# Forward Q and K projections as four column groups of 32 rows, with the memory rows batched over eight segments and Q and K kept token-major in DRAM

## The chip, the cores and the metric

The kernel runs on one core of one Trainium2 chip. The metric is the device time in microseconds (us) of one execution of the whole kernel, forward and backward in one launch. Each run also left one execution taken by the hardware profiler; all readings below are from such executions. "Granted clock" is the share of full speed that the throttle allowed TensorE.

The engines are named as the profile names them: PE is TensorE (PEld its weight loads), DVE is VectorE, ACT is ScalarE, POOL is GpSimd, SP is SyncE, whose queue here does nothing but issue DMAs.

## The reference

A memory-augmented recurrent attention, a residual, a SwiGLU feed-forward layer, and the gradients of all of it. Only the attention matters here: 64 segments run one after the other, because the first 8 output rows of a segment are the memory rows of the next.

```python
# S=2048 tokens, D=448, H=16 heads, Dh=256, M=8 memory rows, seg_len=32, L=40 rows in a segment
mem = mem0
for s in range(64):
    h = concatenate([mem, x[:, 32*s : 32*s + 32]], axis=1)       # 40 rows
    q = einsum('btd,dhe->bhte', h, Wq); k = ... Wk; v = ... Wv    # each 448 x 4096
    scores = where(mask, einsum('bhqe,bhke->bhqk', q, k) * scale, -1e9)
    p = softmax(scores)
    o = einsum('bhqk,bhke->bhqe', p, v)
    o = einsum('bhte,hed->btd', o, Wo)
    mem = o[:, :8]                                                # the recurrence
    outs.append(o[:, 8:])
h = x + concat(outs);  out = h + swiglu(layernorm(h));  gradients by vjp
```

The memory rows of a segment are known only at the very end of the segment before. The kernel lays the 40 rows out with the memory rows last: the 32 rows `M:L` are 24 tokens and the 8 memory rows, and the 8 rows `0:M` are tokens, which are known long before. That is what the change uses.

## The kernel before

The sequence of one forward segment. Weights are the stationary operand, the 40 rows of the segment the moving one, so Q and K come out with the feature on the partitions and need no transpose:

```python
def wpass(W_sb, s, dst, hb, eng):                     # 64 matmuls in two banks; four calls a segment
    for x in range(2):
        ps = k.ps1()
        for j in range(j0, j0 + 8):
            for kc in range(KC):                      # KC = 4 chunks of 128 rows; the last holds 64, padded with zeros
                nc.tensor.matmul(ps[:, (j-j0)*L:(j-j0+1)*L],                    # L432
                    lhsT=W_sb[:, kc, c*P:(c+1)*P], rhs=hT_roll[:, kc, sl, :], ...)
        k.evac(dst[:, j0:j0+8, 0:L], ...)             # L75 on VectorE, L76 on ScalarE

# one segment s
wpass(Wq_sb, s, qT, 0, "vs"); wpass(Wk_sb, s, kT, 0, "sv"); wpass(Wq_sb, s, qT, 1, "vs")
pS0 = scores(0)                                       # L500 mask, L505 scores
softmax(0, pS0)                                       # L512 to L518, VectorE and ScalarE
wpass(Wk_sb, s, kT, 1, "sv")
value_rows(0)                                         # L527, V: 8 matmuls 128x512 in two column groups, x4
pS1 = scores(1); softmax(1, pS1)
value_rows(1); transposed_p(0); value_rows(2)         # L536
values(0); transposed_p(1); value_rows(3)             # L548
out_proj(0, 8); values(1); out_proj(8, MC)            # L561, four column groups of 32 rows
to_s = nc.scalar.copy(out=om[0:64, :], in_=pO[64:P, 0:256])        # L589: "om", once a segment
to_v = nc.vector.tensor_tensor(out=om2[0:64, :], ...)              # L590
... nc.tensor.transpose(...)                                       # L596, memory rows turned
to_v = nc.vector.tensor_copy(out=hT_roll[..., SEG:L], ...)         # L597, into the next segment's rows
# (cut) stores for the backward: feature-major Q and K, padded from 40 to 64 columns, 512 KB each
nc.gpsimd.dma_start(out=dr["QT"][s], in_=qT...)
nc.sync.dma_start(out=dr["KT"][s], in_=kT...)
nc.sync.dma_start(out=dr["VG"][s], in_=Vs)
```

In the backward, each segment loads Q, K and V with transposing DMAs, and every 16th segment stores a block of memory-row gradients (`DHb`) on the queue that also loads `DH` for the layer norm's backward:

```python
def load_seg(s):
    load_v(s)                                                       # transposing load of VG
    nc.sync.dma_start_transpose(out=Q_sb, in_=dr["QT"][s])
    nc.sync.dma_start_transpose(out=K_sb, in_=dr["KT"][s])
    ...
# each backward segment: ... nc.vector.tensor_copy(out=om[:, 0:224], in_=pH[:, 0:224])   # L990 "omb"
if jm == 0:                                                         # jm = s % 16
    nc.sync.dma_start_transpose(out=dhx, in_=dmr...)                # L1009
    nc.gpsimd.dma_start(out=dr["DHb"][r0:r0+P, :], in_=dhx...)      # L1011
if r == 0:                                                          # r = s % 4
    ...
    nc.gpsimd.dma_start(out=dh_h, in_=dr["DH"][rows, c0:c0+224])    # L1052, in ln_bwd (L260)
```

`with tc.issue_after(x):` places what is inside it behind instruction `x` in the scheduler's order; otherwise a list scheduler puts the instructions of each engine, DMAs included, in one order. That an issue stands behind an earlier one of its engine is seen in the timelines below: in the changed kernel a store whose data was ready at 335.80 us was issued on SyncE's queue at 352.84, behind a DMA whose buffer came free at 349.60.

## Time and profile before

Before the prediction the kernel's time was 3364.26 us (median of three runs, 3356.36 to 3373.26). I cut the profiled execution into stages by the start of ScalarE's copy L589 (one per forward segment) and VectorE's L990 (one per backward segment):

| stage, kernel before | us |
|---|---|
| start to the end of segment 0 | 54.5 |
| 63 forward segments | 1111.1, mean 17.64, median 16.97, lowest 16.12 |
| feed-forward layer, to the first backward segment | 398.9 |
| 63 backward segments | 1084.7, mean 17.22, median 16.76 |
| weight gradients and the rest | 721.4 |

The page's first and second parts and its instruction queue: busy time and its share of the span, then busy tenths in 40 equal slices, the granted clock in tenths, and packets, MB and share of the 16 DMA engines.

```profile
PE 2994.7 (89%) x56532; PEld 2021.4 (60%) x56532; DVE 1306.7 (39%) x3309; ACT 1036.2 (31%) x2501; POOL 727.8 (22%) x1507
...
PE   5888888988988869886999999999999589999998
...
PEclk8999999999999989997999999999999799999999
...
q8 instruction: 442, 7.24, 0.9%
```

TensorE is busy in eight or nine tenths of most slices, so the work on TensorE and what TensorE waits for set the time. One forward segment without a disturbance, from the timeline of PE (start, duration, line, output<-input, shape of the operands, matmuls in the group, and in brackets the idle time before and who ended it):

```profile
97.34 4.96 PE L432 MATMUL psf<-arA,arW 128*128 128x40 bf16 x192 [0.27 <-DVE arA L597]
102.14 0.23 PE L500 MATMUL psf<-arB,ident 128*128 128x160 bf16 x1
...
102.67 1.77 PE L432 MATMUL psf<-arA,arW 128*128 128x40 bf16 x64
104.37 1.05 PE L527 MATMUL psf<-arW,arA 128*64 128x512 bf16 x8
...
110.49 1.49 PE L561 MATMUL po<-arW,arA 128*32 128x256 bf16 x48
112.97 0.23 PE L596 MATMUL psf<-ident,arB 64*128 64x64 bf16 x2 [0.98 <-DVE arB L590]
113.46 0.31 PE L432 MATMUL psf<-arA,arW 128*128 128x40 bf16 x6 [0.26 <-DVE arA L597]
```

Subtract starts, not durations, since the records of two groups overlap (97.34 + 4.96 = 102.30, and the next group starts at 102.14): Q and K take 4.80 + 1.70 = 6.50 us, and the segment 113.46 − 97.34 = 16.12 us. This is the lowest of the 63. The mean is 1.5 us more, and the list of waits of PE between 60 and 1160 us (us in total, times, longest) says what part of that is:

```profile
PE psf L596 <- DVE arB L590: 49.9, 50, 1.6
PE psf L432 <- issue: 40.4, 24, 4.7
```

"issue" is time in which TensorE waited for nothing that the profile shows. In the backward (1564 to 2649 us), the wait of PE and then of DVE:

```profile
PE po L972 <- DVE arA L75: 23.6, 15, 7.3
```

```profile
DVE arB L260 <- DMA arB<-DH: 49.3, 15, 7.5
```

### The profile page before, as it was taken

Reading aid. Unit: us, or ns where it says so; the run is one execution under the profiler, and the core shown is the slowest. Engines: PE = TensorE matmul, PEld = TensorE weight load, DVE = VectorE, ACT = ScalarE, POOL = GpSimd, SP = SyncE. Lnnn points to the kernel's source line nnn. Section 1 sums busy time; section 2 is a strip of 40 time slices with the busy share of each in tenths; the row PEclk is TensorE's granted clock in tenths of the full one; section 3 lists DMA queues with packets and bytes.
Section 4 is the critical chain, followed back from the end, with each engine's and each line's share of the span. In section 5 each row is a group of like instructions: output and inputs, shape, how many; then the busy total and the mean of one; then the engine's idle time right before and its main releaser. Section 6 shows DMA issues by size and latency. Waiting matters only on the chain.

```text
span 3370.6 us, 124942 instructions
## 1 busy us (share of the span) xinstructions
PE 2994.7 (89%) x56532; PEld 2021.4 (60%) x56532; DVE 1306.7 (39%) x3309; ACT 1036.2 (31%) x2501; POOL 727.8 (22%) x1507
## 2 busy tenths in 40 slices
PE   5888888988988869886999999999999589999998
PEld 4666666676766646664666666666666344444443
DVE  4344344344344357773444444444444201111110
ACT  2333333333333323332333333333333101020110
POOL 3222222122121212121222222122211212112111
PEclk8999999999999989997999999999999799999999
DMA  7656865777665698987777878887877967979952
GB/s 271 188 158 182 220 165 159 182 183 204 175 183 159 211 240 198 200 209 238 162 169 160 168 158 180 157 168 163 174 164 171 287 190 210 201 183 195 198 146 69
DMA packets 998890, 623.49 MB, mean 185 GB/s; under 512 B 900868, under 2 KB 912788, under 8 KB 995860
## 3 DMA queue, kind: packets, MB, share of 16 engines
q1 hardware_dynamic: 921428, 361.57, 51.6%
q0 software_dynamic: 76928, 253.93, 22.8%
q8 instruction: 442, 7.24, 0.9%
q14 instruction: 92, 0.75, 0.1%
HBM read 125.38 MB, written 271.52 MB: 118 GB/s over the span
## 4 chain that ended last, share of the span: by engine, by line
PE 68%; issue 10%; DVE 9%; DMA 7%; ACT 3%; POOL 1%; SPq 1%; ACTq 0%; POOLq 0%; DVEq 0%
PE psf L432 12%; PE po L972 8%; PE psf L1149 8%; PE psf L929 5%; PE psf L527 4%; PE psf L906 4%; PE po L561 3%; PE psf L1170 3%; PE fx L1031 3%; PE psf L710 2%; PE fx L800 2%; PE psf L994 2%; PE fx L1154 2%; DVE arA L75 2%; PE psf L548 2%
## 5 line engine op out<-in xcount | busy, mean ns | idle before, releaser
L76 ACT CAST arA<-psf 128x320 bf16<-128x320 f32 (+5 forms) x1267 | 519.1, 425 | 1491.0 <-PE psf L432 390.1
L75 DVE CAST arA<-psf 128x320 bf16<-128x320 f32 (+5 forms) x1093 | 489.2, 464 | 1016.6 <-PE psf L1149 259.2
L432 PE MATMUL psf<-arA,arW 128*128 128x40 bf16 x16384 | 450.8, 181 | 81.1 <-issue 41.8
L432 PEld LDWEIGHTS <-arW 128*128 128x128 bf16 x16384 | 439.9, 97 | 90.3 <-issue 67.4
L972 PE MATMUL po<-arW,arA 128*32 128x448 bf16 x6144 | 360.9, 365 | 47.8 <-DVE arA L75 43.6
L527 PE MATMUL psf<-arW,arA 128*64 128x512 bf16 x2048 | 275.6, 394 | 4.7 <-DMA arW<-in_A_Wv_dram 2.8
L1149 PE MATMUL psf<-arW,arA 128*128 128x512 bf16 x1030 | 259.5, 379 | 0.0
L972 PEld LDWEIGHTS <-arA 128*32 128x32 bf16 x6144 | 155.1, 98 | 168.5 <-DVE arA L75 46.5
L1149 PEld LDWEIGHTS <-arA 128*128 128x128 bf16 x1440 | 136.0, 98 | 164.8 <-issue 13.7
L929 PEld LDWEIGHTS <-arW 128*128 128x128 bf16 x8192 | 213.8, 96 | 28.9 <-issue 28.9
L929 PE MATMUL psf<-arA,arW 128*128 128x40 bf16 x8192 | 217.9, 180 | 10.1 <-DVE arA L998 5.1
L710 PE MATMUL psf<-arW 128*128 128x256 bf16 x1344 | 155.9, 277 | 50.3 <-DMA arW<-arW 38.5
L710 PEld LDWEIGHTS <-arW 128*128 128x128 bf16 x1344 | 133.1, 99 | 75.0 <-issue 37.3
L527 PEld LDWEIGHTS <-arA 128*64 128x64 bf16 x2048 | 109.6, 113 | 64.1 <-issue 12.3
L561 PE MATMUL po<-arW,arA 128*32 128x192 bf16 (+1 forms) x4096 | 136.7, 262 | 5.9 <-DMA arW<-in_A_Wo_dram 5.0
L76 ACT CAST arB<-psf 40x160 bf16<-40x160 f32 (+3 forms) x448 | 120.9, 270 | 35.3 <-DVE arB L75 25.6
L906 PEld LDWEIGHTS <-arW 128*128 128x128 bf16 x2048 | 88.9, 101 | 66.3 <-issue 63.4
L939 ACT COPY arA<-psf 128x1024 bf16<-128x1024 bf16 x128 | 123.3, 1015 | 2.2 <-PE psf L938 0.4
L561 PEld LDWEIGHTS <-arA 128*32 128x32 bf16 x4096 | 96.1, 96 | 40.7 <-DVE arB L75 20.2
L1170 PEld LDWEIGHTS <-arW 128*128 128x128 bf16 x606 | 60.1, 99 | 98.7 <-DMA arW<-X_o 36.6
L75 DVE CAST arB<-psf 40x160 bf16<-40x160 f32 (+3 forms) x384 | 108.5, 296 | 22.5 <-PE psf L536 22.5
L906 PE MATMUL psf<-arB,arW 128*128 128x80 bf16 x2048 | 100.0, 204 | 16.1 <-DVE arB L956 6.1
(272 smaller groups left out, 3848.9 us busy)
## 6 DMA issues: line engine op xcount, KB each, us to landing
QT<-arA POOLq DMA_DIRECT2D x64, 512.0 KB, 4.6
KT<-arA SPq DMA_DIRECT2D x64, 512.0 KB, 4.2
VG<-arA SPq DMA_DIRECT2D x64, 512.0 KB, 3.8
X_o<-arA POOLq DMA_DIRECT2D x40, 512.0 KB, 5.5
X_v<-arA POOLq DMA_DIRECT2D x32, 512.0 KB, 6.7
X_k<-arA POOLq DMA_DIRECT2D x32, 512.0 KB, 4.1
X_q<-arA POOLq DMA_DIRECT2D x32, 512.0 KB, 4.4
arW<-X_o SPq DMA_DIRECT2D x30, 512.0 KB, 14.5
```

Source lines behind the costliest of these rows:

```text
L75: return nc.vector.tensor_copy(out=out, in_=in_)
L76: return nc.scalar.copy(out=out, in_=in_)
L432: nc.tensor.matmul(ps[:, (j - j0) * L:(j - j0 + 1) * L], lhsT=W_sb[:, kc, c * P:(c + 1) * P], rhs=hT_roll[:, kc, sl, :], start=(kc == 0), ...
L527: nc.tensor.matmul(pV[64 * g:64 * g + 64, 0:512], lhsT=hT_flat[:, kc, sl * L:sl * L + 64], rhs=Wv_sb[:, kc, n * 512:(n + 1) * 512], start= ...
L561: nc.tensor.matmul(pO[32 * q:32 * q + 32, 0:w], lhsT=xblk[:, j, r * SEG:(r + 1) * SEG], rhs=Wo_sb[:, cj(j), 256 * dh:256 * dh + w], start= ...
L710: nc.tensor.matmul(ps[:, f2 * 256:(f2 + 1) * 256], lhsT=Wt[:, kc, c * P:(c + 1) * P], rhs=xT[:, kc, :], start=(kc == 0), stop=(kc == KC - 1))
L906: nc.tensor.matmul(ps[b][:, i * 2 * L:(i + 1) * 2 * L], lhsT=lhs[:, cl, :], rhs=rhs_bd[:, cl // 2, :, :].rearrange("p g n -> p (g n)"), st ...
L929: nc.tensor.matmul(pss[b][:, jj * L:(jj + 1) * L], lhsT=WoT_sb[:, kc, c * P:(c + 1) * P], rhs=do_roll[:, kc, sl, :], start=(kc == 0), stop ...
L939: nc.scalar.copy(out=dO_sb[:, 8 * hf:8 * hf + 8, :], in_=ph.rearrange("p (c n) -> p c n", n=P))
L972: nc.tensor.matmul(pH[32 * (j % 4):32 * (j % 4) + 32, 0:D], lhsT=blk[nm][:, j, r * SEG:(r + 1) * SEG], rhs=WT[:, cj(j), :], start=(nm == " ...
L1149: nc.tensor.matmul(pa[2 * kc + g][:, 0:w], lhsT=lhs_of(b)[:, kc * P:(kc + 1) * P], rhs=rhs_of(b, g), start=(b == 0), stop=(b == nblk - 1), ...
L1170: nc.tensor.matmul(pa[i][:, 0:D], lhsT=lhs_of(b, i), rhs=rhs_of(b), start=(bi == 0), stop=(bi == len(nblk) - 1))
```

## The change

The intent is to make Q and K with fewer TensorE instructions. The 32 rows `M:L` become the stationary operand, four copies of it in four column groups of the array, and the weights the moving one, 512 columns at a time; the last, half-filled chunk of the contraction runs Q's part in rows 0 to 63 and K's part in rows 64 to 127 of the array together (in the trace after, the eight such matmuls of a block start within 23 ns). The result is token-major and has to be turned back by 16 TensorE transposes. The other 8 rows, known early, are projected for 8 segments at once with 64 moving columns, spread over the segments before, and GpSimd copies 8 of the columns into each segment's Q and K. V's last chunk is halved the same way. In DRAM, Q and K are now stored token-major (`T1q`, `T1k` per segment, `T0q`, `T0k` per 8 segments), so that the backward loads them with plain DMAs in place of transposing ones, and V is stored in 80 rows in place of 128.

The core of the diff (cut: allocation, start-up, V, the order within the segment):

```diff
-    def wpass(W_sb, s, dst, hb, eng):   # (shown above)
+    qk_st = A(15, 2, 2, 512)                                   # one staging buffer for all segments
+    def qk_rows(s, b):
+        banks = [k.ps1(), k.ps1()]
+        for w in range(2):
+            for kc in range(KC - 1):
+                for q in range(4):                             # four column groups
+                    nc.tensor.matmul(banks[w][32*q:32*q+32, :], lhsT=hT_roll[:, kc, sl, M:L],
+                                     rhs=(Wq_sb, Wk_sb)[w][:, kc, col(q, b)], ...)          # L465
+        for q in range(4):
+            for w in range(2):                                 # half chunks: row group w, column group q
+                last = nc.tensor.matmul(banks[w][32*q:32*q+32, :], lhsT=hT_roll[64*w:64*w+64, KC-1, sl, M:L],
+                                        rhs=Wqk3[64*w:64*w+64, col(q, b)], ...)             # L469
+        for w in range(2):
+            k.evac(qk_st[:, w, b, :], banks[w][:], "vs"[w])
+    def qk_turned(s, b):                                       # 8 transposes, L479, two copies
+        ...
+    def rest_rows(s):                                          # GpSimd: 8 columns into Q and K, L424
+        ...
+            qk_rows(s, 0); qk_rows(s, 1)
+            qk_turned(s, 0); value_rows(0)
+            pS0 = scores(0); softmax(0, pS0)
+            qk_turned(s, 1); value_rows(1); value_rest(0)      # L578, half chunks of V L586
+            ...
+            out_proj(8, MC)
+            if bm < NSEG // 8 - 1:                             # bm, bu = divmod(s, 8)
+                for u in (...): rest_unit(bm + 1, u)           # 32 matmuls of 64 columns, L413
-        nc.gpsimd.dma_start(out=dr["QT"][s], in_=qT.rearrange("p c n -> p (c n)"))
-        nc.sync.dma_start(out=dr["KT"][s], in_=kT.rearrange("p c n -> p (c n)"))
+        for w, nm in enumerate("qk"):
+            nc.sync.dma_start(out=dr["T1" + nm][s], in_=qk_st[:, w]...)                     # L672
-        nc.sync.dma_start(out=dr["VG"][s], in_=Vs)
+        for g in range(2):
+            nc.sync.dma_start(out=dr["VG"][s, L*g:L*g+L], in_=Vs[64*g:64*g+L, :])           # L675
+        if bu == 2 + bm % 2:
+            for w, nm in enumerate("qk"):
+                ot = stg()
+                nc.sync.dma_start_transpose(out=ot..., in_=R_b[bm % 2][w]...)               # L685
+                nc.gpsimd.dma_start(out=dr["T0" + nm][bm], in_=ot)
@@ load_seg (backward)
-        nc.sync.dma_start_transpose(out=Q_sb, in_=dr["QT"][s])
-        nc.sync.dma_start_transpose(out=K_sb, in_=dr["KT"][s])
+        for nm, T_sb in (("q", Q_sb), ("k", K_sb)):
+            t1 = dr["T1" + nm][s]...; t0 = dr["T0" + nm][s // 8]...
+            for g in range(2):
+                for src, i0, i1 in ((t1[g], M, L), (t0[s % 8, g], 0, M)):
+                    nc.sync.dma_start(out=T_sb[64*g+i0:64*g+i1]..., in_=src)
```

## The prediction

> **What bounds the kernel.** The chain of waits is TensorE for 68% and "issue" for 10%. By ScalarE's copy of the output projection (one per segment), the forward recurrence runs to 1166 us: segment 0 ends at 55 us, 63 more take 17.6 us each. FFN runs to about 1545, backward to 2640, weight gradients to the end.
>
> **An undisturbed forward segment** (timeline from 97.3 us) takes 16.1 us of TensorE issue time:
>
> | part | us |
> |---|---|
> | Q and K, 256 matmuls 128x40 at 25 to 26.6 ns | 6.5 |
> | V, 32 matmuls | 4.0 |
> | mask, scores, P transposes, values | 2.3 |
> | output projection, 64 in four column groups | 1.9 |
> | wait for om, turn of memory rows | 1.5 |
>
> The mean is 1.5 us more. The list of waits gives L432 40 us of "issue" (24 stalls, up to 4.7 us). The instruction queue moved 7.24 MB, about 64 bytes per TensorE instruction; I read the stalls as fetch falling behind 512 instructions in 6.5 us.
>
> **After, per segment.**
> - Q and K: two blocks of six rounds of four 32x512 matmuls. The backward's four-group 448-column matmuls take 204 ns a round (43 in 2.19 us), so I estimate 230 ns at 512. The eight half-chunk matmuls: 0.35 us, estimated. Sum 3.5. [...] this trace shows column groups only (48 output-projection matmuls in 1.40 us).
> - 16 transposes at 61 ns (L938): 1.0.
> - Other 8 rows: 32 matmuls of 64 columns, about 35 ns each (between 25 at 40 columns and 46 at 80): 1.1, largely inside the om wait.
> - V: 3.6.
>
> TensorE instructions fall from 840 to 550 a segment, and their fastest burst goes.
>
> Against it: VectorE gains two casts 128x512 (685 ns), two bf16 copies (about 400), two V casts and a remainder copy, and loses four casts at 489: +2 us, between two softmaxes whose chain from scores to P is 2.16 us. Laid end to end with trace durations, TensorE waits for V's bank (0.25), P (0.3, then 0.9 for the second half), value copies (0.6) and the first rows (0.5). I get 16.2 us undisturbed (15.9 to 16.7): no shorter than now. The gain should come from lost stalls: 16.6 on average, a forward of 1100 us, saving 60 to 70.
>
> **Backward.** Two of three large transposing loads per segment become plain loads of 2 KB rows. Q and K have about 15 us to land. VectorE's 42 us of waits for DH loads and TensorE's 16 us behind VectorE may shrink: 10 us. FFN and gradients: unchanged.
>
> **Prediction:** 3285 us, 80% range 3215 to 3345. Faster by over 2%: 0.57; within 2%: 0.36; slower: 0.07.
>
> **What would show it.** Segment spacing 16.2 to 16.8; Q/K rounds near 230 ns; half chunks under 0.5 us a block; forward "issue" under 15 us; a wait near 0.9 us of the second P transposes for VectorE; backward shorter by 0 to 20 us.
>
> **What would make it wrong.** GpSimd now copies the other 8 rows into Q and K on its in-order queue, behind DMA issues that wait for transposes (140 us today); if late, scores wait. Row groups that serialize add up to 1 us a segment. If the stalls have another cause, they stay: "same". If VectorE overlaps better, 15.5 us a segment and near 3220.

## The result, and the profile after

The changed kernel took 3275.43 us (median of four runs, 3272.35 to 3282.10), the kernel before in the same rounds 3368.76 (3356.36 to 3374.21). A ratio in this document is the mean time of one kernel's fast runs over the mean of the other's fast runs of the same rounds, so it is not quite the ratio of the medians quoted. It is 0.9731 here, with a 95% interval of 0.9697 to 0.9764: faster by 2.7%. The time is 10 us from the predicted 3285 and inside the range.

The stages, cut the same way (by L654 and L1074), show that it was not reached in the predicted manner:

| stage | before | after | measured change | predicted change |
|---|---|---|---|---|
| to the end of segment 0 | 54.5 | 59.3 | +4.8 | in the next line |
| 63 forward segments | 1111.1 | 1065.6 | −45.6 | −60 to −70 |
| lowest forward segment | 16.12 | 15.11 | −1.01 | none (16.2) |
| mean forward segment | 17.64 | 16.91 | −0.72 | about −1.0 (16.6) |
| forward segments over 18.5 us | 17 | 10 | −7 | no number given |
| feed-forward layer | 398.9 | 392.7 | −6.2 | 0 |
| 63 backward segments | 1084.7 | 1035.0 | −49.7 | −10 (0 to −20) |
| weight gradients and the rest | 721.4 | 727.8 | +6.4 | 0 |

How far may one such profile be trusted? A second profile of the changed kernel (the control run below) had a forward of 1056.5, a feed-forward stage of 401.8 and a backward of 1032.8. The kernel before repeats less well: its forward, unchanged in four of the runs below, took 1104.5 to 1118.4 us there, and its backward, unchanged in e7_before_fwd_plain, 1092.9 against 1084.7. So I don't read a difference under 14 us between single forward stages, nor one under 10 us between single feed-forward or backward stages.

The same lines of the page after:

```profile
PE 2935.2 (89%) x47442; PEld 1763.0 (54%) x47442; DVE 1393.8 (42%) x3497; ACT 1030.0 (31%) x2437; POOL 761.7 (23%) x1716
...
PE   6889898988988869995999999999999499999998
...
PEclk9999999999999989997999999999999799999999
...
q8 instruction: 372, 6.09, 0.8%
```

TensorE's busy time fell by only 60 us. An undisturbed segment of the changed kernel, again from PE's timeline:

```profile
541.48 1.48 PE L465 MATMUL psf<-arW,arA 128*32 128x512 bf16 x24 [0.27 <-DVE arA L664]
542.89 0.41 PE L469 MATMUL psf<-arW,arA 64*32 64x512 bf16 x8
543.23 1.48 PE L465 MATMUL psf<-arW,arA 128*32 128x512 bf16 x24
544.63 0.41 PE L469 MATMUL psf<-arW,arA 64*32 64x512 bf16 x8
544.98 0.62 PE L479 MATMUL psf<-ident,arA 128*128 128x128 bf16 x8
...
552.11 0.28 PE L596 MATMUL fx<-ident,arB 128*40 128x40 bf16 x8 [0.66 <-DVE arB L568]
...
554.81 1.10 PE L413 MATMUL fx<-arA,arW 128*128 128x64 bf16 x32
555.87 0.20 PE L660 MATMUL psf<-ident,arB 64*128 64x64 bf16 x1
...
556.59 0.40 PE L465 MATMUL psf<-arW,arA 128*32 128x512 bf16 x4 [0.27 <-DVE arA L664]
```

Both Q/K blocks take 544.98 − 541.48 = 3.50 us. The other rows (L413) fill the 1.06 us in which the kernel before waited 0.98 us for "om", and the memory rows' turn (L660) follows them with no idle time. All of one undisturbed segment, start to start, each row summed over its groups in the timeline:

| part, us | before | after | predicted for after |
|---|---|---|---|
| Q and K matmuls | 6.50 | 3.50 | 3.5 |
| transposes of Q and K | – | 1.09 | 1.0 |
| V | 3.98 | 4.13 | 3.6 |
| mask and scores | 0.97 | 0.68 | |
| P transposes and values | 1.15 | 1.29 | |
| output projection | 2.05 | 1.98 | |
| other 8 rows | – | 1.06 | 1.1 |
| wait for om | 0.98 | – | |
| turn of the memory rows, with its wait of 0.27 | 0.49 | 0.72 | |
| other idle time of PE | – | 0.66 | 2.05 (V bank 0.25, P 0.3 and 0.9, value copies 0.6) |
| sum | 16.12 | 15.11 | 16.2 |

The list of waits of PE in the forward (60 to 1120 us), and then that of DVE (59 to 1125 us):

```profile
PE psf L479 <- DVE arA L75: 62.6, 12, 8.3
PE fx L596 <- DVE arB L568: 35.9, 63, 0.7
...
PE psf L660 <- DVE arB L655: 10.2, 10, 1.4
```

```profile
DVE arA L75 <- DMA T1q<-arA: 67.5, 8, 11.1
...
DVE arB L521 <- DMA arB<-Oh: 21.5, 3, 7.5
```

No "issue" is left in PE's list for the forward. But there is a new largest entry: the transposes of Q and K wait 62.6 us in 12 places, up to 8.3 us, for VectorE's copies into the staging buffer, and VectorE waits 67.5 us in 8 places for the DMA that stores the staging buffer (`T1q<-arA`) to be done with it. The segments agree: the changed kernel's lie at 15.1 to 17.4, except indices 2, 9, 17, 25, 33, 41 and 49 (8 apart, 23.7 to 25.1 us) and 19, 35 and 51 (22.6 to 22.7 us).

What happens at index 17 (346.3 to 370.4 us)? SyncE's timeline (the queue's own; the second number is the time the issue took):

```profile
344.46 1.46 SPq L506 DMA_TRANSPOSE arA<-in_A_Wo_dram  x1
349.66 3.13 SPq L685 DMA_TRANSPOSE arA<-arW  x1
352.84 1.22 SPq L672 DMA_DIRECT2D T1q<-arA  x1
```

and VectorE's:

```profile
356.49 1.29 DVE L75 CAST arA<-psf 128x512 bf16<-128x512 f32 x2 [8.51 <-DMA T1q<-arA]
```

The chain of waits through this stretch names the same steps in order: the store of a transposed piece of Wo (`To<-arA`, from 346.55) must land before its buffer is free; only then, at 349.60, does SyncE issue the transposing DMA of the other rows (L685) into that buffer; the staging buffer's store T1q stands behind it and is issued at 352.84; it lands at 356.40, and VectorE copies again. The data of that store had been ready since 335.80, when VectorE's last copy of the segment before into the staging buffer ended: the store stood 17 us in line, and not for its data. The stall costs more than itself. The view by windows (stretch, its length, the busy time of PE, PEld, DVE, ACT and POOL, then the granted clock, the DMA share and GB/s) shows the clock after it:

```profile
351.00:357.00 6.00, 1.31 (x28) 0.37 (x20) 0.51 (x1) 0.00 (x0) 0.54 (x1) 0.86 0.99 237
357.00:358.50 1.50, 1.26 (x10) 0.88 (x12) 0.87 (x3) 1.07 (x2) 1.50 (x6) 0.50 1.10 202
```

The records have the clock at 0.5 from 355.32 for 6.83 us, 4.91 us of them after TensorE had gone on at 357.24. The first eight transposes there (L479) take 1.13 us, where the undisturbed segment above has 0.62. All 21 low stretches of the forward before and all 11 of the forward after lie at half clock and last 3.4, 6.8 or 10.2 us (82 and 75 us in sum).

In the backward, the entries shown of before have shrunk (PE, then DVE, 1517 to 2552 us), and no segment is over 18.5 us, where seven were:

```profile
PE po L1056 <- DVE arA L75: 6.1, 14, 0.8
```

```profile
DVE arB L262 <- DMA arB<-DH: 31.8, 15, 2.6
```

The low-clock time in the backward fell from 51.2 to 10.2 us.

### The profile page after: what moved, and what is told of

Read it like the earlier page. It is cut to its first block, busy times and chain, and to the rows that moved or that the text cites. A ratio compares the mean times of both kernels' runs of the same rounds, so it can differ in the third digit from the quotient of the medians.

```text
span 3280.3 us, 108129 instructions
## 1 busy us (share of the span) xinstructions
PE 2935.2 (89%) x47442; PEld 1763.0 (54%) x47442; DVE 1393.8 (42%) x3497; ACT 1030.0 (31%) x2437; POOL 761.7 (23%) x1716
## 4 chain that ended last, share of the span: by engine, by line
PE 60%; DMA 14%; DVE 12%; issue 9%; ACT 2%; SPq 2%; POOL 1%; ACTq 0%; POOLq 0%; DVEq 0%
PE psf L1233 8%; PE po L1056 7%; PE psf L1013 5%; PE psf L465 4%; PE psf L990 4%; DVE arA L75 4%; PE psf L1254 3%; PE po L622 3%; PE fx L1115 3%; PE psf L578 2%; PE fx L879 2%; PE psf L789 2%; PE psf L479 2%; PE fx L1238 2%; PE psf L1078 2%
## 5 line engine op out<-in xcount | busy, mean ns | idle before, releaser
L75 DVE CAST arA<-psf 128x256 bf16<-128x256 f32 (+5 forms) x1029 | 494.1, 499 | 948.0 <-PE psf L1233 258.9
L76 ACT CAST arA<-psf 128x64 bf16<-128x64 f32 (+4 forms) x947 | 375.7, 415 | 1206.7 <-PE psf L1233 256.5
L1056 PEld LDWEIGHTS <-arA 128*32 128x32 bf16 x6144 | 152.6, 97 | 148.1 <-DVE arA L75 34.5
L1013 PEld LDWEIGHTS <-arW 128*128 128x128 bf16 x8192 | 213.2, 96 | 23.9 <-issue 23.9
L1233 PEld LDWEIGHTS <-arA 128*128 128x128 bf16 x1440 | 135.9, 98 | 164.8 <-issue 13.8
L1013 PE MATMUL psf<-arA,arW 128*128 128x40 bf16 x8192 | 216.6, 180 | 5.3 <-DVE arA L1082 5.1
L465 PE MATMUL psf<-arW,arA 128*32 128x512 bf16 x3072 | 193.9, 385 | 13.0 <-DVE arA L664 13.0
L789 PEld LDWEIGHTS <-arW 128*128 128x128 bf16 x1344 | 133.4, 99 | 71.6 <-issue 49.5
L622 PE MATMUL po<-arW,arA 128*32 128x256 bf16 (+1 forms) x4096 | 140.9, 263 | 7.2 <-DMA arW<-in_A_Wo_dram 3.6
L479 PE MATMUL psf<-ident,arA 128*128 128x128 bf16 x1024 | 88.2, 233 | 63.4 <-DVE arA L75 62.6
L990 PEld LDWEIGHTS <-arW 128*128 128x128 bf16 x2048 | 87.5, 100 | 68.5 <-issue 58.8
L465 PEld LDWEIGHTS <-arA 128*32 128x32 bf16 x3072 | 70.5, 96 | 90.6 <-DVE arA L664 18.8
L1254 PEld LDWEIGHTS <-arW 128*128 128x128 bf16 x606 | 60.3, 100 | 107.9 <-DMA arW<-X_o 43.3
L76 ACT COPY arA<-psf 128x512 bf16<-128x512 bf16 (+2 forms) x136 | 79.2, 583 | 110.8 <-DVE arA L75 108.6
L479 PEld LDWEIGHTS <-arA 128*128 128x128 bf16 x1024 | 67.3, 104 | 80.2 <-DVE arA L75 66.2
L622 PEld LDWEIGHTS <-arA 128*32 128x32 bf16 x4096 | 93.4, 96 | 29.0 <-DVE arA L75 11.6
```

The lines of the kernel that those rows point to most:

```text
L75: return nc.vector.tensor_copy(out=out, in_=in_)
L76: return nc.scalar.copy(out=out, in_=in_)
L465: nc.tensor.matmul(banks[w][32 * q:32 * q + 32, :], lhsT=hT_roll[:, kc, sl, M:L], rhs=(Wq_sb, Wk_sb)[w][:, kc, col(q, b)], start=(kc == 0) ...
L479: nc.tensor.transpose(pt[:, w * 512 + i * P:w * 512 + (i + 1) * P], qk_st[:, w, b, i * P:(i + 1) * P], ident[:, :])
L622: nc.tensor.matmul(pO[32 * q:32 * q + 32, 0:w], lhsT=xblk[:, j, r * SEG:(r + 1) * SEG], rhs=Wo_sb[:, cj(j), 256 * dh:256 * dh + w], start= ...
L789: nc.tensor.matmul(ps[:, f2 * 256:(f2 + 1) * 256], lhsT=Wt[:, kc, c * P:(c + 1) * P], rhs=xT[:, kc, :], start=(kc == 0), stop=(kc == KC - 1))
```

## The experiments

Three questions were open: where the forward's gain went, why the undisturbed segment got shorter, and where four fifths of the backward's gain came from. Twelve runs were made: eleven edited kernels, and the changed kernel once more. Where a result is wrong, the text says so, and the run is used for its time alone. The stage times of all of them:

| run | forward, 63 segments | median segment | segments over 18.5 | backward | us, median | ratio to before |
|---|---|---|---|---|---|---|
| before | 1111.1 | 16.97 | 17 | 1084.7 | 3368.76 | 1 |
| after | 1065.6 | 15.25 | 10 | 1035.0 | 3275.43 | 0.9731 |
| e15_after_again | 1056.5 | 15.26 | 10 | 1032.8 | 3277.59 | 0.9744 |
| e1_scalar_store | 1013.8 | 15.51 | 5 | 1038.7 | 3233.08 | 0.9593 |
| e6_store_first | 1013.9 | 15.25 | 4 | 1033.5 | 3229.15 | 0.9615 |
| e8_store_first_late_residual | 996.6 | 15.12 | 1 | 1035.9 | 3216.53 | 0.9572 |
| e10_no_other_rows | 1016.0 | 15.26 | 7 | 1032.2 | 3227.21 (once) | – |
| e7_before_fwd_plain | 1073.7 | 16.90 | 6 | 1092.9 | 3333.78 | 0.9921 |
| e2_back_turned | 1053.0 | 15.25 | 10 | 1074.9 | 3307.02 | 0.9809 |
| e4_v128 | 1066.4 | 15.26 | 10 | 1039.8 | 3296.89 | 0.9775 |
| e3_before_plain | 1108.8 | 16.99 | 16 | 1055.6 | 3344.06 | 0.9930 |
| e13_before_no_qk_loads | 1114.6 | 16.97 | 18 | 1048.1 | 3328.86 | 0.9905 |
| e14_before_plain_short | 1118.4 | 16.97 | 21 | 1054.9 | 3352.19 | 0.9950 |
| e16_before_late_dhb | 1104.5 | 16.96 | 18 | 1058.4 | 3347.60 | 0.9955 |

The runs of the kernel before lay between 3357 and 3369 us in the median.

### Where the forward's gain went

**The store on another queue.** My theory: the long segments come from T1q and T1k standing behind transposing DMAs on SyncE's queue. In this run of the changed kernel, ScalarE issues those stores.

```diff
-            nc.sync.dma_start(out=dr["T1" + nm][s], in_=qk_st[:, w]...)
+            nc.scalar.dma_start(out=dr["T1" + nm][s], in_=qk_st[:, w]...)
```

> The changed kernel, with the two stores of the staged Q and K rows issued by ScalarE instead of SyncE. Theory S: in the changed kernel seven forward segments take 23 to 25 us because the single staging buffer of Q and K cannot be written again until its store has landed, and the store stands in SyncE's in-order queue behind transposing loads that wait for a buffer. Then those segments fall to 15 to 17 us, the three near 22.7 us (VectorE waiting for the residual's fetch, as in the kernel before) stay, and the time falls by 45 to 60 us, to about 3220; ScalarE's issuing may take back up to 20 us. Rival G, the risk named in the prediction (GpSimd copies the other 8 rows too late): the long segments stay and the time stays within 10 us of 3275. Rival D (the transposing of the other rows loads the DMA engines, whatever the order): also unchanged.

The result was right, with 3233.08 us (3229.73 to 3235.91) and a ratio to before of 0.9593 (0.955 to 0.9636). The forward fell by 51.8 us against the first profile after and by 42.7 against the second. The seven segments fell to between 15.0 and 18.6 us, where the theory said 15 to 17. But not all went as expected: the three near 22.7 us, which should have stayed, fell to 15.5 to 15.8, and other long ones came (indices 4, 16, 34 and 48, 18.7 to 22.1 us). So the scheduler's order changed elsewhere too, and the total fell by 42 us, less than the 45 to 60 expected. The median segment grew from 15.25 to 15.51. ScalarE spends 326 and 399 ns (medians) on the two issues, and TensorE's list has a new wait for ScalarE's copies (L413, 31.0 us in 43 places); that the issues are what lengthened the segment fits this, but is not isolated. The theory held for its seven segments, and this cure has its own price.

**The store first, on the same queue.** Here the queue stays, and only the order changes: the transposing DMA of the other rows is issued behind the segment's own store.

```diff
-            nc.sync.dma_start(out=dr["T1" + nm][s], in_=qk_st[:, w]...)
+            t1_out = nc.sync.dma_start(out=dr["T1" + nm][s], in_=qk_st[:, w]...)
 ...
+                with tc.issue_after(t1_out.ins):
                     nc.sync.dma_start_transpose(out=ot..., in_=R_b[bm % 2][w]...)
```

> The changed kernel with one order fixed on SyncE's queue: the two transposing loads of the other rows' Q and K stand behind the same segment's stores of the staged Q and K, nothing else moves. Theory S (single staging buffer whose store waits behind those loads in the queue): six or seven of the long segments fall to 15 to 18 us, the segment median stays at 15.25 (no ScalarE issue cost as in the run with ScalarE stores, which had 15.5), and the time falls by 45 to 65 us, to 3210 to 3230. Rival D (load of the DMA engines by those transposes): the same transposes still run, a little later, so the long segments stay, and the time stays within 15 us of 3275.

The result was right: 3229.15 us (3225.72 to 3237.47), 0.9615 (0.9584 to 0.9646). PE's and DVE's lists of waits in the forward (57 to 1071 us):

```profile
PE psf L479 <- DVE arA L75: 22.2, 6, 7.8
```

```profile
DVE arA L75 <- DMA T1q<-arA: 16.6, 3, 10.7
```

The wait fell from 62.6 to 22.2 us and the forward from 1065.6 and 1056.5 to 1013.9. Segments 9, 25 and 41 went to 15.3 us, and 17, 33 and 49 to 17.3 to 17.5; only index 2, in the start-up, stayed at 25.1. SyncE's timeline at index 17 (334.8 to 352.3 us in this run) now has both stores before the two transposing DMAs:

```profile
341.52 0.35 SPq L672 DMA_DIRECT2D T1k<-arA  x1
341.97 0.39 SPq L672 DMA_DIRECT2D T1q<-arA  x1
342.46 5.70 SPq L686 DMA_TRANSPOSE arA<-arW  x2
```

This run is the cleaner proof, as one order was edited and the three segments of the residual stayed: six of the seven fell by 6.5 to 9.8 us each. (That e1_scalar_store won the same 42 to 52 us is in part chance: it also lost its residual segments, and paid in its median and in four new long ones.) That is the place where the gain went. SyncE's traces show how: in the changed kernel the store that had its data at 335.80 was held until 352.84 by a neighbour that hadn't its buffer before 349.60; in this run the two stores of the same index are issued at 341.52 and 341.97, before the neighbour's 342.46. A second staging buffer might make the order unnecessary. It would add 4 KB a partition to the 199.25 KB of the kernel's three arenas; no run has it.

**And the residual later.** The segments 19, 35 and 51 were untouched by this (21 to 22.3 us). VectorE's list has 21.5 us in three waits for `arB<-Oh`, the attention output fetched back for the residual. The kernel before had the same three (19.5 us, longest 6.8), so they are not of the change. In this run the fetch and the addition skip the first of their places after a block of 16 segments.

```diff
+ (the edit of e6_store_first)
-        if due and jm % 3 == 1:                     # fetch
+        if due and jm % 3 == 1 and jm > 1:
-        if due and jm % 3 == 0 and jm > 0:          # residual
+        if due and jm % 3 == 0 and jm > 3:
```

> The run before it, and the residual's fetch and addition moved three segments later in each group of 16 (fetch at 4, 7, 10, 13, addition at 6, 9, 12, 15, was 1, 4, 7, 10 and 3, 6, 9, 12). Theory R: the three segments of about 22.7 us that both kernels have at the fifth place of a group come from VectorE standing in line behind an addition whose fetched row has not landed; then they fall to about 16 and a further 12 to 20 us go, to 3195 to 3215. Rival: another wait takes their place at the seventh segment and nothing is gained.

The result was right: 3216.53 us (six runs, 3206.10 to 3226.52), 0.9572 (0.9542 to 0.9603). The three segments went to 15.1 us, and one long segment is left, index 2 (27.4 us), in the start-up. The further gain is 12.6 us between the medians, at the low end of the 12 to 20 expected, with the total 1.5 us above the range; the intervals of the two ratios overlap. That the residual's place is a cure is shown; it is not the only one, since these three segments were short in e1_scalar_store and e10_no_other_rows too, whose residual was not touched. The low-clock time of the forward is 13.7 us. PE's wait at L479 in the forward (57 to 1054 us):

```profile
PE psf L479 <- DVE arA L75: 8.4, 2, 8.2
```

This is the fastest version of all, ahead of both kernels. In it the mean segment is 15.82 us, and 63 undisturbed segments of 15.11 (951.9 us) leave 44.7 us of disturbance, where the changed kernel has 113.7 (104.6 in the control) and the kernel before 95.5 over its own 1015.6 (88.9 to 102.8 in the four other profiles with its forward). Seen thus, the change did not make the disturbances smaller, rather somewhat larger, and the whole forward gain came from the shorter undisturbed segment.

**The control.** The unchanged changed kernel, once more.

> The changed kernel once more, unchanged, on this chip: a control for how far a profile's stages differ between runs. 3275 within 10 us; forward 1066, backward 1035, each within 5 us.

It took 3277.59 us (3273.48 to 3281.66), 0.9744 (0.9708 to 0.9781). The total repeats within 2.2 us; the forward differed by 9 us, more than I expected, which is why the differences above are given against both profiles.

### What of the shorter segment was hidden

**No other rows.** The changed kernel without the projection of the other rows, except in the first block. The result is wrong.

```diff
-            if bm < NSEG // 8 - 1:
+            if bm == 0:
```

> The changed kernel without the 32 matmuls and two copies per segment that make the other 8 rows, from segment 8 on (their values are stale, the result wrong on purpose). If they hide in the wait for the memory rows, the segment median stays within 0.15 us of 15.25. If they cost their 1.1 us, it falls to about 14.2.

Executed once: 3227.21 us. The median segment stayed at 15.26 us although 1.06 us of matmuls were gone. The list of waits (60 to 1070 us) says where the time went:

```profile
PE psf L660 <- DVE arB L655: 47.7, 48, 1.4
```

That is the wait for om again, 48 times 1.0 us, where the changed kernel has it 10 times; its first three and its last eight segments have no other rows to do. So the other rows are free, as predicted. The forward as a whole was shorter all the same (1016.0), because the long segments were: the seven at 18.9 to 26.8 us, and the three of the residual at 15.1. Why they were, this run does not tell, and I take nothing from its total.

### The lost "issue" stalls

I read the 40.4 us of "issue" in the kernel before as late instruction fetch. This is an inference: the trace shows the packets, not what TensorE waits for. The instruction queue q8 moved 442 packets in 7.24 MB, 16 KB each, for 2 · 56,532 = 113,064 instructions of PE and PEld, 255.8 a packet; after, 372 packets for 94,884, 255.1 a packet. In the trace before, each of the 24 stalls of L432 ended 1.25 to 1.63 us after such a packet landed, so I call the reading well supported. If other DMAs delay the packets, then the transposing DMAs of the forward (weights and blocks for the backward) might do it. In this run of the kernel before, they are plain ones of the same size. The result is wrong.

```diff
-                nc.sync.dma_start_transpose(out=ot..., in_=blk...)
+                nc.sync.dma_start(out=ot, in_=blk...)
-            nc.sync.dma_start_transpose(out=o4[:, 0:3, 0:n], in_=Ws[i0:i0 + n, 0:3 * P])      # and two more
+            nc.sync.dma_start(out=o4[:, 0:3, 0:n], in_=k.Wq2[0:P, 0:3 * n]...)
```

> The kernel before, with the forward's transposing loads of weights and of the attention output replaced by plain copies of the same bytes (wrong gradients on purpose); TensorE's instructions are unchanged. Theory C (TensorE's stalls in the forward need both a fast instruction rate and instruction packets delayed by transposing DMA): TensorE's issue waits on the Q and K line in the forward fall from 40 us to under 12, and the time by 20 to 45 us. Rival F (the burst of 512 instructions outruns the fetch whatever the DMA does): the issue waits stay near 40 us and the time within 12 us of 3366.

3333.78 us (3327.39 to 3338.35), 0.9921 (0.989 to 0.9952). The "issue" of L432 (60 to 1128 us):

```profile
PE psf L432 <- issue: 18.6, 21, 2.8
```

From 40.4 to 18.6 us. Four other profiles with the forward of the kernel before have 32.3 to 39.2 us (longest 2.7 to 3.2), so the total is clear of the spread, and the longest stall is not. 18.6 lies between the two expectations. (The forward fell by 37 us, more than these 22; what the rest was, the run does not tell.) The transposing DMAs have a part in the stalls, though by which way is not shown: the plain ones may also have let the buffers come free sooner. The rest remains at the rate of 256 matmuls of 25 to 26.6 ns. That the changed kernel has none is shown by its list, and by those of all the runs made from it; that the fewer instructions are the reason is argued, not shown.

### The backward

**Turned loads back.** The changed kernel with two transposing loads for Q and K per segment, of the size of those before, from another tensor. The result is wrong.

```diff
-            (the four plain loads of T1 and T0 for each of Q and K)
+            nc.sync.dma_start_transpose(out=T_sb, in_=dr["X_o"][s // 4][:, 2048 * (nm == "k"):2048 * (nm == "k") + 2048])
```

> The changed kernel with Q and K of the backward loaded by two transposing loads of 512 KB per segment again, as in the kernel before (from another tensor of the same shape, so the gradients are wrong on purpose). Theory T: the backward's gain of about 48 us comes from these two loads having gone. Then the backward's segments go back from 16.4 to about 17.2 us, long segments of 19 to 25 us come back, and the time rises by 35 to 55 us, to about 3320. Rival V (the shorter load of V, 80 rows for 128, made the gain) and rival O (the order of the heads or memory layout made it): the backward stays near 16.4 us and the time near 3275.

3307.02 us (3301.84 to 3310.15), 0.9809 (0.9772 to 0.9846). The backward went from 1035.0 to 1074.9, with six segments over 18.5 us again, and the total rose by 32 us. PE's wait for VectorE's copies (1510 to 2584 us) came back by half:

```profile
PE po L1052 <- DVE arA L75: 14.8, 13, 5.8
```

So 40 of the backward's 50 to 52 us came back; the total's 32 us are a little under the 35 to 55 expected. The 40 us are not the loads' alone: with the transposing loads the order of GpSimd's queue came back too, as shown below.

**V's 128 rows back.** The changed kernel with the store and the load of V as before.

```diff
-              VG=dt("VG", [NSEG, 2 * L, W2])
+              VG=dt("VG", [NSEG, P, W2])
-        for g in range(2):
-            nc.sync.dma_start(out=dr["VG"][s, L * g:L * g + L], in_=Vs[64 * g:64 * g + L, :])
+        nc.sync.dma_start(out=dr["VG"][s], in_=Vs)
(and load_v, vT and its one use as before)
```

> The changed kernel with V stored and loaded as before, 128 rows in place of 80. Theory T: the backward keeps nearly all of its gain, the time rises by 0 to 12 us. Rival V: it rises by 35 us or more.

The result was right: 3296.89 us (3283.89 to 3303.36), 0.9775 (0.9733 to 0.9817). The backward rose by 5 us, which a single profile doesn't resolve, so V's length is not the cause of its gain. The total, though, rose by 21 us between the medians, more than the 0 to 12 expected; the intervals of the two ratios overlap, and no single stage differs by more than two profiles of one kernel do. What made it is open.

**Plain loads in the kernel before.** The reverse of e2_back_turned. Its output is wrong, which doesn't matter for the time.

```diff
-        nc.sync.dma_start_transpose(out=Q_sb, in_=dr["QT"][s])      # and K
+        nc.sync.dma_start(out=Q_sb.rearrange("p a b -> p (a b)"), in_=dr["QT"][s])
```

> The kernel before with the backward's Q and K loads made plain instead of transposing (same bytes, wrong gradients on purpose). Theory T: the backward's segments fall from 17.2 to about 16.4 us and the time by 35 to 55 us, to about 3320. Rival V or O: no change, 3365 within 10 us.

3344.06 us (3338.39 to 3363.73), 0.993 (0.9883 to 0.9978). The backward fell by 29 us, and the median time by 22, less than the 35 to 55 expected. Of the changed kernel's gain 21 to 23 us were still missing. Two runs asked whether it was the bytes: these plain loads carry 128 padded rows, those of the changed kernel only the 80 in use.

**No loads, and short loads.** Both are the kernel before. Their outputs are wrong, which doesn't matter for the times.

```diff
 e13_before_no_qk_loads
+        if s == NSEG - 1:
             nc.sync.dma_start_transpose(out=Q_sb, in_=dr["QT"][s])      # and K
 e14_before_plain_short
+        n = P if s == NSEG - 1 else 2 * L
+        nc.sync.dma_start(out=Q_sb[0:n]..., in_=dr["QT"][s][0:n])       # and K
```

> The kernel before, with Q and K of the backward loaded for the first segment only (stale afterwards, gradients wrong on purpose): the floor for what these loads can cost. Theory T: the backward takes about as long as in the changed kernel, 1030 to 1045 us (was 1085), and the kernel is 35 to 55 us faster. Rival V: with the long V load still there, it stays above 1055 us.

> The kernel before, with plain loads of Q and K of 80 of their 128 rows (320 KB each, as many bytes as the changed kernel loads; wrong gradients on purpose). The plain loads of all 512 KB left the backward at 1056 us against 1040 in the changed kernel with the long V. If the bytes made these 16 us, the backward is near 1040 here; if V or the stalls' chance made them, it stays near 1055.

Without any loads the backward is 1048.1 (−37, 3 us above the range expected), with short ones 1054.9, the same as with long ones (1055.6). The bytes are not the cause: even without a single byte the kernel before doesn't reach 1035. The times were 3328.86 (3322.18 to 3346.46; 0.9905, 0.986 to 0.995) and 3352.19 (3335.92 to 3354.69; 0.995, 0.9901 to 1.0).

What did stay in all of these were three segments, indices 14, 46 and 62, of 20 to 22 us (21.5, 21.0 and 25.5 in the kernel before, 16.2 to 16.5 in the changed one). There GpSimd's queue is in another order. Its timeline in the kernel before:

```profile
1807.99 0.55 POOL L1011 DMA_DIRECT2D DHb<-arA  x1 [4.80 <-DMA arA<-arA]
1808.52 0.55 POOL L1052 DMA_DIRECT2D arB<-DH  x1
```

and in the changed kernel, where the load of DH is ahead of the store:

```profile
1753.46 0.55 POOL L1136 DMA_DIRECT2D arB<-DH  x1 [2.76 <-DVE arB L262]
...
1761.11 0.54 POOL L1095 DMA_DIRECT2D DHb<-arA  x1
```

The code of the two is the same here. In the kernel before the store of DHb stands 4.80 us for a transposing DMA, and the load of DH, which VectorE's layer norm needs, stands behind it. In e2_back_turned, which differs from the changed kernel in the loads of Q and K alone, the store is ahead again:

```profile
2016.79 0.54 POOL L1091 DMA_DIRECT2D DHb<-arA  x1 [4.20 <-DMA arA<-arA]
2017.32 0.55 POOL L1132 DMA_DIRECT2D arB<-DH  x1
```

**The store of DHb later.** The last run makes that one move in the kernel before. The result is right.

```diff
         if jm == 0:
             nc.sync.dma_start_transpose(out=dhx, in_=dmr...)
-            nc.gpsimd.dma_start(out=dr["DHb"][r0:r0 + P, :], in_=dhx...)
 ...
-            nc.gpsimd.dma_start(out=OUT1[rows, :], in_=xn_t)
+            out1 = nc.gpsimd.dma_start(out=OUT1[rows, :], in_=xn_t)
+            if jm == 0:
+                with tc.issue_after(out1.ins):
+                    nc.gpsimd.dma_start(out=dr["DHb"][r0:r0 + P, :], in_=dhx...)
```

> The kernel before, right results, with one move in the backward: the store of the transposed memory-row gradients (DHb, every 16th segment), which on GpSimd's in-order queue stands ahead of the load of DH for the layer norm and waits 4.8 us for a transposing load, is issued behind that layer norm's output instead. Theory (the three long backward segments of 20 to 25 us, indices 14, 46 and 62, are this store blocking the DH load, and the change removed them by an accident of the scheduler's order): those three segments fall to about 16.5 us, VectorE's wait for DH in the backward (41.8 us in the kernel before) falls by 10 or more, and the backward falls from 1084.7 to 1066 to 1075 us; total ratio 0.995. Rival (the long segments come from something else that the change touched, such as the loads of Q and K): they stay at 20 to 25 us and the backward stays at 1080 to 1090.

The three segments went to 16.3, 16.5 and 16.1 us. VectorE's wait for DH in the backward (1560 to 2650 us) fell from 49.3 by 10.5 us:

```profile
DVE arB L260 <- DMA arB<-DH: 38.8, 16, 6.5
```

The backward went from 1084.7 to 1058.4, by more than the 10 to 18 us I expected and more than these three segments (18.8 us over 16.4 us each); the rest is within what two profiles of an unchanged backward differ by. The time was 3347.60 us (3342.68 to 3352.75), 0.9955 (0.9929 to 0.9981), about 15 us; the stage after the backward was 8 us longer (729.5), for which I have no cause. The theory held: the change got this part of its gain by an order that the scheduler happened to choose.

This also settles how the two causes share the gain. The backward of every run, split into the four segments with a store of DHb (indices 14, 30, 46 and 62) and the other 59:

| run | store of DHb, load of DH | 4 segments, us | other 59, us |
|---|---|---|---|
| before | store first | 85.7 | 999.1 |
| e7_before_fwd_plain (backward unchanged) | store first | 84.5 | 1008.4 |
| e3_before_plain | store first | 81.2 | 974.4 |
| e14_before_plain_short | store first | 80.9 | 974.0 |
| e13_before_no_qk_loads | store first | 80.6 | 967.5 |
| e16_before_late_dhb | load first | 65.8 | 992.6 |
| e2_back_turned | store first | 80.4 | 994.5 |
| after | load first | 65.8 | 969.3 |
| e15_after_again | load first | 65.3 | 967.5 |

The 59 follow the loads of Q and K (about 1000 us with transposing ones, 967 to 974 with plain ones or none), and the four follow the order (81 to 86 against 65 to 66). Of the 49.7 us, 30 lie in the 59 and 20 in the four. PE's wait for VectorE's copies (L972, 23.6 us in the kernel before) goes mostly with the order: 6.6 us in e16_before_late_dhb, but 16.2 to 17.5 in the three runs of the kernel before with plain loads or none. Why the scheduler's order changed with the loads in the changed kernel, but not in the kernel before (e3_before_plain, e13_before_no_qk_loads), is open.

## Why the prediction was right or wrong, point by point

The total was right within 10 us because two errors were of opposite sign: the forward saved less than predicted and the backward more. That is luck. Term by term:

- **The parts of Q and K: right.** 3.50 us for both blocks (3.5 predicted), rounds of four column groups every 216 ns (230 predicted), half-chunk parts 0.34 us a block (0.35). The eight half-chunk matmuls start within 23 ns, 3.3 ns apart, so row and column groups do run together here, and the risk of row groups that serialize did not come; in the trace before I had seen column groups only, and the 0.35 was my estimate. A block repeats every 1.75 us (543.23 − 541.48), where seven rounds of 216 ns would be 1.51; what the other 0.24 us are, no run separates.
- **The other rows hidden in the wait for om: right.** 1.06 us (1.1 predicted), and e10_no_other_rows shows that taking them away leaves the median segment where it was.
- **"I get 16.2 us undisturbed (15.9 to 16.7): no shorter than now": wrong.** It is 15.11 against 16.12, outside the range. The mis-sized term is the sum of TensorE's waits. I laid V bank 0.25, P 0.3 and 0.9, value copies 0.6 and first rows 0.5, 2.55 us, end to end. The trace has 0.66 for P's second half and 0.27 for the first rows, 0.93 together. I had put together durations of VectorE's chain as though TensorE had no V work to set beside it. Against this V took 4.1 us, not the 3.6 assumed.
- **"The gain should come from lost stalls: 16.6 on average, a forward of 1100 us, saving 60 to 70": wrong in its mechanism, and too large.** The old stalls were lost: the list of waits in the forward goes from 40.4 us of "issue" at L432 to none, as predicted (under 15). But the mean is 16.91 and the forward ended 41 us earlier (1165.6 to 1124.8). New stalls of 62.6 us took their place: the one staging buffer `qk_st` had to be stored before the next segment could write it, and its store stood on SyncE's queue behind transposing DMAs that waited for their own buffers. e6_store_first, which frees the store by one order alone, wins 43 to 52 us of the forward. The prediction had looked for late work on GpSimd's queue ("GpSimd now copies the other 8 rows into Q and K on its in-order queue"). That risk did not come: PE's and DVE's lists have no wait for GpSimd's copy. The right danger was on the other in-order queue.
- **"10 us" for the backward: mis-sized.** It was 50 to 52, outside the 0 to 20. The mechanism named, plain loads in place of transposing ones, was right and was worth about 30 us: in the 59 segments without a store of DHb it is 25 us by e3_before_plain and, reversed, by e2_back_turned, and 30 in the change itself. I had costed it as a part of two waits in the list, and had left out the clock after such waits: low-clock time in the backward fell from 51.2 to 10.2 us, and half a clock over 41 us is up to 20 us of matmuls, by my estimate from that difference and from L972 in the kernel before, where four matmuls take 373 ns at half clock and 189 at full (medians, start to start). A second part was not foreseen at all: the store of DHb moved behind the load of DH, which by e16_before_late_dhb is worth 20 us in the four segments that have it. The two parts add up to the 50 us.
- **"FFN and gradients: unchanged": right as far as the profiles resolve.** They measured −6 and +6 us. The stage after the backward took 728 us in the changed kernel and 730 in the control and in e16_before_late_dhb, against 721 before; the cause of these 6 to 9 us is open.

The forward's gain thus came from the part of the prediction that gave as a reason for being wrong: "If VectorE overlaps better, 15.5 us a segment and near 3220." It needed the staging store first: e6_store_first comes to 3229.15. e8_store_first_late_residual comes to 3216.53, but its move of the residual would be open to the kernel before as well.

## What to carry to other kernels

When a change adds a buffer that is both written each iteration and stored by a DMA, place its store on its in-order queue as carefully as the arithmetic: look at what stands ahead of the store and what that waits for. Here that one order was worth 43 to 52 us of the forward (e6_store_first). An undisturbed iteration and the disturbances are two sums, to be read apart: here the disturbance went from 95 to 105 to 114 us while the iteration fell by 1.01 us, and only the first number pointed at cures worth another 1.6% together. When an edit is to test one cause, look in its trace whether the scheduler has also changed another order; e1_scalar_store and e2_back_turned both did. When waits are laid end to end in an estimate, put beside each one the independent work that the engine can do in it.
